# Attention with tokens as rows: the product in 64-row tiles, the norm per token on VectorE, x transposed afterwards

## The chip, the cores and the metric

The kernel runs on one core of a Trainium2 chip. The metric is device time in microseconds of one execution; the median of three runs is compared. A profiled execution gives the trace, whose times start at the first instruction. Engines are named as in the profile: PE is TensorE's matmuls, PEld its weight loads, DVE is VectorE, ACT ScalarE, POOL GpSimd, SP the engine that issues the loads and stores.

## The reference

q, k, v have the shape (8, 8, 576, 64): batch, heads, tokens, head dimension. A linear attention without softmax is followed by a root-mean-square norm per token and head, and then a feed-forward block with a gate over 4608 tokens x 512.

```python
kv = np.einsum('bhsd,bhse->bhde', k, v)
out = np.einsum('bhsd,bhde->bhse', q, kv)
rms = np.sqrt(np.mean(out * out, axis=-1, keepdims=True) + 1e-06)
x = (out / rms * g_norm).transpose(0, 2, 1, 3).reshape(B * S, H * D)
g = x @ w_gate                      # 512 -> 1536
result = (g / (1 + exp(-g)) * (x @ w_val)) @ w_out
```

## The kernel before

The 4608 tokens are cut into nine blocks of 512 (`BLK`), four tiles of 128 tokens each (`T`). A batch has 576 tokens, so block n takes its first tokens from batch n-1 and the rest from batch n. Features lie in four pairs of heads (`NS`), 128 rows each.

`Att` is the attention of a block, cut into steps. `load` asks for k and v of one batch (96 partitions, six chunks of 96 tokens) and q. `kv` computes k^T v of a pair of heads: six accumulating matmuls of 64 columns for the head u = 0, which writes PSUM rows 0 to 63, then six for u = 1, which writes rows 64 to 127 (L229). The result goes into a block-diagonal 128 x 128 matrix per pair (L235, L236). `turn_q` transposes q on TensorE, 16 transposes of 128 x 128 (L245), copied out by VectorE (L246). `product` multiplies with the block-diagonal matrix as the weight and 512 tokens as the moving operand (L257), so x comes out with features as rows. ScalarE squares it (L263), VectorE copies it (L264), and a matmul with the 0/1 matrix `head_of` sums the squares of each head into 8 rows (L265). `rms` computes 1/sqrt on 8 x 512 numbers in eleven VectorE instructions (L273 to L285: one scaling, a first guess from the bits, and three Newton steps of three). `scale` spreads the roots, times the gain, over 128 rows by a matmul with 8 rows (L291), and VectorE multiplies (L292). `sums` prepares four sums and differences for `Up`.

The feed-forward block is a seven-product scheme (`Quad`, L332, 256 columns a matmul): `Up` runs six times a block (7 x 4 matmuls each), `Down` once (7 x 12 matmuls). GpSimd prepares differences of weights (L120) and products (L121). Block 0 runs plain matmuls instead (`plain_up` L495, `plain_down` L508), as the weights arrive and are rounded from 64-bit words by ScalarE and VectorE meanwhile (L151 to L164).

All matmuls share one in-order stream on TensorE. Block n+1's attention steps are handed to block n's feed-forward as fillers: the `kv` steps between turns of `Up`, `turn_q` after `Up`, and one of the late steps after each part of `Down`:

```python
            ffn.up(kv)
            for step in kv + turn:
                step()
            ffn.down(late)
```

Block 0's own attention comes first, with only the first weight pieces beside it. The framework plans each engine's order from the program's order, with a cost for each instruction: an instruction whose inputs the plan expects late lets later ones go ahead of it. On the chip, each engine then runs its list in that order. PSUM has eight banks: two each for the pools a, b, c (products of `Quad`) and m (all of the attention).

A float32 matmul shows in the trace as two records, a transpose as one.

Of the kernel before, what the change touches and what calls it, by code (L numbers as in the profile page):

```python
# [18 lines left out]
def kernel(  # L19
# [51 lines left out]
    KT = S // KP  # L71
    eps = 1e-6
# [3 lines left out]
    def pool(name, bufs, **kw):  # L76
        return ctx.enter_context(tc.tile_pool(name=name, bufs=bufs, **kw))

    consts = pool("consts", 1)
    ld_pool = pool("ld", 7)  # L80
    qt_pool = pool("qt", 1)
    sq_pool = pool("sq", 2)
    st_pool = pool("st", 1)
    x_pool = pool("x", 1)
    h_pool = pool("h", 1)
    s_pool = pool("s", 1)
# [2 lines left out]
    o_pool = pool("o", 1)  # L89

    PS = bass.MemoryType.PSUM
    a_psum = pool("a_psum", 2, space=PS)
    b_psum = pool("b_psum", 2, space=PS)
    c_psum = pool("c_psum", 2, space=PS)
    m_psum = pool("m_psum", 2, space=PS)

    ident = consts.tile([P, P], F32, name="ident")
    make_identity(nc, ident)

    head_of = consts.tile([P, NS, H], F32, name="head_of")  # L100
    nc.vector.memset(head_of, 0.0)

    gain = consts.tile([H, NS, P], F32, name="gain")
    nc.vector.memset(gain, 0.0)
    for h in range(H):
        j, u = divmod(h, 2)
        rows = slice(u * D, (u + 1) * D)
        nc.vector.memset(head_of[rows, j, h : h + 1], 1.0)
        nc.gpsimd.dma_start(out=gain[h : h + 1, j, rows], in_=g_norm.rearrange("(o d) -> o d", o=1))

    kvs = [consts.tile([P, NS, P], F32, name=f"kv{i}") for i in range(3)]
    for t in kvs:
        nc.gpsimd.memset(t, 0.0)

    wg = consts.tile([P, NS, FF], F32, name="wg")
    wv = consts.tile([P, NS, FF], F32, name="wv")
# [4 lines left out]
    mul = lambda e, o, a, b: e.tensor_tensor(out=o, in0=a, in1=b, op=OP.mult)  # L121
# [67 lines left out]
    class Att:  # L189


        def __init__(self, n):
            self.n = n
            self.cut = 16 * n

        def load(self):
            n, cut = self.n, self.cut
            self.k, self.v, self.q = [], [], []
            if n < B:
                for j in range(NS):  # L200
                    hs = slice(2 * j, 2 * j + 2)
                    for tiles, src in ((self.k, k), (self.v, v)):
                        t = ld_pool.tile([P, 2 * BLK], F32, name="ld")
                        t = t[0:KP, 0 : 2 * KT * D].rearrange("p (h x) -> p h x", h=2)
                        nc.sync.dma_start(
                            out=t, in_=src[n, hs].rearrange("h (p t) d -> p h (t d)", t=KT)
                        )
                        tiles.append(t.rearrange("p h (t d) -> p h t d", t=KT))
            for i in range(2):
                hs = slice(4 * i, 4 * i + 4)  # L210
                t = ld_pool.tile([P, 2 * BLK], F32, name="ld")
                t = t.rearrange("p (t h d) -> p t h d", t=T, h=4)
                for b, s0, p0, p1 in ((n - 1, S - 4 * cut, 0, cut), (n, 0, cut, P)):
                    if p1 > p0:
                        rows = q[b, hs, s0 : s0 + T * (p1 - p0), :].rearrange("h (p t) d -> p t h d", t=T)
                        for c in range(T):
                            nc.sync.dma_start(out=t[p0:p1, c], in_=rows[:, c])
                self.q.append(t)

        def kv(self, js):  # L220
            if self.n == B:
                return
            if js[0] == 0:
                self.kv_ps = m_psum.tile([P, NS, D], F32, name="m")
            for j in js:
                for u in range(2):
                    rows = slice(u * D, (u + 1) * D)
                    for c in range(KT):
                        nc.tensor.matmul(  # L229
                            self.kv_ps[rows, j, :], lhsT=self.k[j][:, u, c, :], rhs=self.v[j][:, u, c, :],  # L230
                            start=(c == 0), stop=(c == KT - 1),
                        )
            if js[-1] == NS - 1:
                dst, ps = kvs[self.n % 3], self.kv_ps
                nc.scalar.copy(out=dst[0:D, :, 0:D], in_=ps[0:D])  # L235
                nc.vector.tensor_copy(out=dst[D:P, :, D:P], in_=ps[D:P])  # L236

        def turn_q(self, js):
            if js[0] == 0:
                self.qt = qt_pool.tile([P, NS, T, P], F32, name="qt")  # L240
            for j in js:
                ps = m_psum.tile([P, T, P], F32, name="m")
                hs = slice(2 * (j % 2), 2 * (j % 2) + 2)
                for t in range(T):
                    nc.tensor.transpose(ps[:, t, :], self.q[j // 2][:, t, hs, :], ident)  # L245
                nc.vector.tensor_copy(out=self.qt[:, j], in_=ps)  # L246

        def product(self, js):
            n, cut = self.n, self.cut
            if js[0] == 0:  # L250
                self.x = x_pool.tile([P, NS, BLK], F32, name="x")
                self.r_ps = m_psum.tile([P, BLK], F32, name="m")
            for j in js:
                ps = m_psum.tile([P, T, P], F32, name="m")
                for b, p0, p1 in ((n - 1, 0, cut), (n, cut, P)):
                    if p1 > p0:
                        nc.tensor.matmul(  # L257
                            ps[:, :, p0:p1], lhsT=kvs[b % 3][:, j, :], rhs=self.qt[:, j, :, p0:p1],
                            start=True, stop=True,
                        )  # L260
                ps = ps.rearrange("p t c -> p (t c)")
                sq = sq_pool.tile([P, BLK], F32, name="sq")
                nc.scalar.activation(out=sq, in_=ps, func=ACT.Square)  # L263
                nc.vector.tensor_copy(out=self.x[:, j, :], in_=ps)  # L264
                nc.tensor.matmul(  # L265
                    self.r_ps[0:H, :], lhsT=head_of[:, j, :], rhs=sq, start=(j == 0), stop=(j == NS - 1)
                )

        def rms(self):


            z = st_pool.tile([H, BLK], F32, name="z")
            nc.vector.tensor_scalar(  # L273
                out=z, in0=self.r_ps[0:H, :], scalar1=1.0 / D, scalar2=eps, op0=OP.mult, op1=OP.add
            )
            y = st_pool.tile([H, BLK], F32, name="y")
            nc.vector.tensor_scalar(
                out=y.bitcast(I32), in0=z.bitcast(I32), scalar1=-0.5, scalar2=float(0x5F3759DF),
                op0=OP.mult, op1=OP.add,
            )  # L280
            a = st_pool.tile([H, BLK], F32, name="a")
            for _ in range(3):
                nc.vector.scalar_tensor_tensor(out=a, in0=y, scalar=-0.5, in1=y, op0=OP.mult, op1=OP.mult)
                nc.vector.tensor_tensor(out=a, in0=a, in1=z, op=OP.mult)
                nc.vector.scalar_tensor_tensor(out=y, in0=a, scalar=1.5, in1=y, op0=OP.add, op1=OP.mult)  # L285
            self.y = y

        def scale(self, js):
            for j in js:
                ps = m_psum.tile([P, BLK], F32, name="m")  # L290
                nc.tensor.matmul(ps, lhsT=gain[:, j, :], rhs=self.y, start=True, stop=True)  # L291
                nc.vector.tensor_tensor(out=self.x[:, j, :], in0=self.x[:, j, :], in1=ps, op=OP.mult)  # L292

        def sums(self):
            x = self.x
# [6 lines left out]
            sub(nc.vector, self.s4, a12, a21)  # L302

        def steps(self):
            lo, hi = (0, 1), (2, 3)
            kv = [lambda: self.kv(lo), lambda: self.kv(hi)]
            turn = [lambda: self.turn_q(lo), lambda: self.turn_q(hi)]
            late = [
                lambda: self.product(lo), lambda: self.product(hi), self.rms,
                lambda: self.scale(lo), lambda: self.scale(hi),  # L310
            ]
            return kv, turn, late + ([self.sums] if self.n else [])

# [4 lines left out]
    class Quad:  # L318


        def __init__(self, steps):
            self.steps = steps
            self.ps = {}
# [124 lines left out]
    class Ffn:  # L448
# [2 lines left out]
            self.h = h_pool.tile([P, NF, BLK], F32, name="h")  # L451

        def store(self, o, t):
            rows = out[BLK * self.n : BLK * (self.n + 1), :].rearrange("(p t) d -> p t d", t=T)
            nc.sync.dma_start(out=rows[:, t : t + 2, :], in_=o)

        def up(self, fill):
# [141 lines left out]
```

## Time and profile before

| | |
|---|---|
| median of 3 runs | 1233.29 us (1233.04 to 1233.48) |
| profiled execution | 1231.31 us, span 1229.5 us |
| PE busy | 1188.3 us (97%) |
| PEld busy | 911.1 us (74%) |
| DVE, ACT, POOL busy | 439.6, 242.0, 403.2 us |
| mean granted TensorE clock | 0.982 |
| DMA | 57.50 MB, mean 47 GB/s |

Busy time counts every moment in which an instruction of that engine runs. Matmuls are pipelined and their records overlap, so the distance between the starts of two records says what one of them costs the stream. "L229" is line 229 of the kernel. In a group's row stand the line, engine, operation, what is written and read, the shape and the number of records; then busy time and the mean length of one in ns; then the idle time of the engine before them and what ended it.

### The profile page before, as it was taken

The numbers are of one execution on the slowest core, as the hardware profiler recorded it, in microseconds if no ns is written. First come the engines' busy times: TensorE is split into PE (matmuls) and PEld (weight loads), VectorE is DVE, ScalarE is ACT, GpSimd is POOL, SyncE is SP. The second block draws the span as 40 slices with busy tenths as digits, with TensorE's granted clock in tenths as the row PEclk, the third lists the DMA queues.
The fourth block names the chain that finished last, engine by engine and source line by source line (L and its number), as shares of the span: only waits on it lengthen the run. The fifth ranks groups of instructions, "written<-read, shape, count | busy, mean of one in ns | idle before, by whom it ended". The sixth has DMA issues, their size and how long they took to land.

```text
span 1229.5 us, 13554 instructions
## 1 busy us (share of the span) xinstructions
PE 1188.3 (97%) x5504; PEld 911.1 (74%) x5504; DVE 439.6 (36%) x707; ACT 242.0 (20%) x414; POOL 403.2 (33%) x329
## 2 busy tenths in 40 slices
PE   5699999999999999999999999999999999999998
PEld 3144344887788868887888778877887788768887
DVE  3556865213511342225222442135123512352121
ACT  2134420221022201221122102210222022201210
POOL 2000110444234423451344224432444235324550
PEclk8599999999999999999999999999999999999999
DMA  9134550030003000210011000200030000000000
GB/s 288 45 120 140 182 148 17 1 92 20 4 32 92 20 1 35 66 38 10 35 45 49 20 35 19 75 20 18 18 79 1 1 35 1 1 1 35 1 1 35
DMA packets 69533, 57.50 MB, mean 47 GB/s; under 512 B 41056, under 2 KB 65632, under 8 KB 69472
## 3 DMA queue, kind: packets, MB, share of 16 engines
q1 hardware_dynamic: 69216, 56.64, 15.3%
q8 instruction: 44, 0.72, 0.2%
q14 instruction: 17, 0.14, 0.0%
q0 software_dynamic: 256, 0.00, 0.0%
HBM read 47.19 MB, written 9.44 MB: 46 GB/s over the span
## 4 chain that ended last, share of the span: by engine, by line
PE 83%; DVE 2%; POOL 1%; issue 0%; ACT 0%; POOLq 0%
PE b L332 41%; PE c L332 19%; PE a L332 10%; PE m L257 3%; PE m L291 2%; PE m L265 2%; PE m L229 2%; PE b L508 2%; PE m L245 1%; POOL t L120 1%; POOL h L121 1%; DVE qt L246 0%; DVE wv L119 0%; DVE u L119 0%; DVE wv L120 0%; DVE s L119 0%
## 5 line engine op out<-in xcount | busy, mean ns | idle before, releaser
L120 POOL TENSOR_TENSOR t<-wv 128x512 f32<-128x512 f32 x48 | 63.4, 1322 | 402.1 <-PE b L332 153.4
L120 POOL TENSOR_TENSOR t<-wg,wv 128x512 f32<-128x512 f32 x96 | 123.0, 1284 | 188.4 <-PE c L332 100.7
L120 POOL TENSOR_TENSOR t<-wo 128x512 f32<-128x512 f32 x72 | 91.3, 1268 | 149.9 <-PE c L332 99.8
L119 DVE TENSOR_TENSOR s<-h 128x256 f32<-128x256 f32 x48 | 20.4, 425 | 306.6 <-POOL h L121 306.6
L332 PE MATMUL b<-x,t 128*128 128x256 f32 x384 | 91.3, 381 | 0.8
L332 PE MATMUL b<-x,wg 128*128 128x256 f32 x384 | 92.0, 382 | 0.0
L332 PE MATMUL b<-x,wv 128*128 128x256 f32 x384 | 90.7, 379 | 0.0
L332 PE MATMUL b<-xs,t 128*128 128x256 f32 x384 | 90.7, 379 | 0.0
L332 PE MATMUL c<-xs,t 128*128 128x256 f32 x384 | 90.7, 379 | 0.0
L332 PE MATMUL c<-xs,wv 128*128 128x256 f32 x384 | 90.7, 379 | 0.0
L332 PE MATMUL a<-x,wg 128*128 128x256 f32 x384 | 90.7, 379 | 0.0
L332 PE MATMUL b<-wo,h 128*128 128x256 f32 x384 | 90.1, 382 | 0.0
L119 DVE TENSOR_TENSOR u<-c,u 128x512 f32<-128x512 f32 x96 | 66.0, 687 | 62.3 <-ACT u L375 62.2
L332 PE MATMUL b<-t,h 128*128 128x256 f32 x384 | 87.0, 383 | 0.8 <-ACT u L437 0.8
L332 PEld LDWEIGHTS b<-t,h 128*128 128x128 f32 x384 | 71.7, 190 | 21.0 <-issue 11.8
L332 PEld LDWEIGHTS b<-wo,h 128*128 128x128 f32 x384 | 70.8, 190 | 16.3 <-issue 7.0
L332 PEld LDWEIGHTS b<-x,t 128*128 128x128 f32 x384 | 72.3, 190 | 12.0 <-issue 2.5
L332 PEld LDWEIGHTS c<-xs,wv 128*128 128x128 f32 x384 | 73.0, 190 | 9.9
L332 PEld LDWEIGHTS b<-xs,t 128*128 128x128 f32 x384 | 73.0, 190 | 9.9
L332 PEld LDWEIGHTS b<-x,wv 128*128 128x128 f32 x384 | 73.0, 190 | 9.9
L332 PEld LDWEIGHTS c<-xs,t 128*128 128x128 f32 x384 | 73.0, 190 | 9.9
L332 PEld LDWEIGHTS a<-x,wg 128*128 128x128 f32 x384 | 73.0, 190 | 9.9
(79 smaller groups left out, 1537.3 us busy)
## 6 DMA issues: line engine op xcount, KB each, us to landing
ld<-in_k_dram SPq DMA_DIRECT2D x32, 288.0 KB, 3.6
ld<-in_v_dram SPq DMA_DIRECT2D x32, 288.0 KB, 3.1
out_dram<-o SPq DMA_DIRECT2D x18, 512.0 KB, 2.6
ld<-in_moe_w_gate_dram SPq DMA_DIRECT2D x12, 512.0 KB, 4.2
ld<-in_moe_w_val_dram SPq DMA_DIRECT2D x12, 512.0 KB, 3.7
ld<-in_moe_w_out_dram SPq DMA_DIRECT2D x12, 512.0 KB, 3.5
ld<-in_q_dram SPq DMA_DIRECT2D x16, 128.0 KB, 2.8
ld<-in_q_dram SPq DMA_DIRECT2D x16, 112.0 KB, 2.7
```

Source lines behind the costliest of these rows:

```text
L119: add = lambda e, o, a, b: e.tensor_tensor(out=o, in0=a, in1=b, op=OP.add)
L120: sub = lambda e, o, a, b: e.tensor_tensor(out=o, in0=a, in1=b, op=OP.subtract)
L121: mul = lambda e, o, a, b: e.tensor_tensor(out=o, in0=a, in1=b, op=OP.mult)
L229: nc.tensor.matmul(self.kv_ps[rows, j, :], lhsT=self.k[j][:, u, c, :], rhs=self.v[j][:, u, c, :], start=(c == 0), stop=(c == KT - 1),)
L245: nc.tensor.transpose(ps[:, t, :], self.q[j // 2][:, t, hs, :], ident)
L257: nc.tensor.matmul(ps[:, :, p0:p1], lhsT=kvs[b % 3][:, j, :], rhs=self.qt[:, j, :, p0:p1], start=True, stop=True,)
L265: nc.tensor.matmul(self.r_ps[0:H, :], lhsT=head_of[:, j, :], rhs=sq, start=(j == 0), stop=(j == NS - 1))
L291: nc.tensor.matmul(ps, lhsT=gain[:, j, :], rhs=self.y, start=True, stop=True)
L332: nc.tensor.matmul(self.ps[name][:, e], lhsT=lhsT, rhs=rhs, start=first and (e, i) == (0, 0), stop=i == self.steps - 1, skip_group_check=True,
L508: nc.tensor.matmul(ps, lhsT=self.h[:, f, P * t : P * (t + 1)], rhs=wo[:, f, :], start=(f == 0), stop=(f == NF - 1),)
```

## The change

In the new form the product is made with tokens as rows. The transposed q of one tile and pair is the weight: 64 rows (one head's features) x 128 tokens; k^T v of that head, 64 x 64, is the moving operand. The heads u = 0 and u = 1 take rows 0 to 63 and 64 to 127, alternate, and write into different PSUM banks. In an odd block the tile in which two batches meet is cut into two halves of 64 tokens. The block's two halves (two tiles each) are worked on one after the other. ScalarE squares, VectorE sums 64 numbers per token and head (`tensor_reduce`), computes the root on 128 x 16 numbers and multiplies. Then x is transposed on TensorE and copied out of PSUM by ScalarE, which applies the gain per row. The matrices `head_of` and the spread gain, their matmuls, the block-diagonal zeros and the copies of x by VectorE are gone. In `kv`, the two heads alternate instruction by instruction. Every second copy of the transposed q goes to ScalarE; the copy of k^T v is one ScalarE instruction. A tile is now 128 consecutive tokens instead of every fourth, so q's loads are 4 or 5 a block, each for all heads, and the store writes rows of 2 KB. Pool a has one bank, pool m three.

```diff
-    st_pool = pool("st", 1)
+    st_pool = pool("st", 2)
+    xt_pool = pool("xt", 2)
...
-    a_psum = pool("a_psum", 2, space=PS)
+    a_psum = pool("a_psum", 1, space=PS)
...
-    m_psum = pool("m_psum", 2, space=PS)
+    m_psum = pool("m_psum", 3, space=PS)
...
-    head_of = consts.tile([P, NS, H], F32, name="head_of")
-    nc.vector.memset(head_of, 0.0)
-
-    gain = consts.tile([H, NS, P], F32, name="gain")
-    nc.vector.memset(gain, 0.0)
-    for h in range(H):
-        j, u = divmod(h, 2)
-        rows = slice(u * D, (u + 1) * D)
-        nc.vector.memset(head_of[rows, j, h : h + 1], 1.0)
-        nc.gpsimd.dma_start(out=gain[h : h + 1, j, rows], in_=g_norm.rearrange("(o d) -> o d", o=1))
-
-    kvs = [consts.tile([P, NS, P], F32, name=f"kv{i}") for i in range(3)]
-    for t in kvs:
-        nc.gpsimd.memset(t, 0.0)
+    gain = consts.tile([P, 1], F32, name="gain")
+    for u in range(2):
+        nc.gpsimd.dma_start(out=gain[u * D : (u + 1) * D], in_=g_norm.rearrange("(d o) -> d o", o=1))
+
+    kvs = [consts.tile([P, NS, D], F32, name=f"kv{i}") for i in range(3)]
...
-            self.cut = 16 * n
+
+            self.cut, half = divmod(n, 2)
+            self.split = half * D
+
+        def parts(self, t):
+
+            n, first = self.n, P * t - D * self.n
+            if t < self.cut:
+                return [(n - 1, S + first, 0, P)]
+            if t == self.cut and self.split:
+                return [(n - 1, S - D, 0, D), (n, 0, D, P)]
+            return [(n, first, 0, P)]
...
-                hs = slice(4 * i, 4 * i + 4)
-                t = ld_pool.tile([P, 2 * BLK], F32, name="ld")
-                t = t.rearrange("p (t h d) -> p t h d", t=T, h=4)
-                for b, s0, p0, p1 in ((n - 1, S - 4 * cut, 0, cut), (n, 0, cut, P)):
-                    if p1 > p0:
-                        rows = q[b, hs, s0 : s0 + T * (p1 - p0), :].rearrange("h (p t) d -> p t h d", t=T)
-                        for c in range(T):
-                            nc.sync.dma_start(out=t[p0:p1, c], in_=rows[:, c])
-                self.q.append(t)
+                ld = ld_pool.tile([P, 2 * BLK], F32, name="ld").rearrange("p (t h d) -> p t h d", t=2, h=H)
+                for t in range(2):
+                    for b, s0, p0, p1 in self.parts(2 * i + t):
+                        nc.sync.dma_start(
+                            out=ld[p0:p1, t], in_=q[b, :, s0 : s0 + p1 - p0, :].rearrange("h p d -> p h d")
+                        )
+                    self.q.append(ld[:, t].rearrange("p (j u) d -> p j (u d)", u=2))
...
             for j in js:
-                for u in range(2):
-                    rows = slice(u * D, (u + 1) * D)
-                    for c in range(KT):
+                for c in range(KT):
+                    for u in range(2):
                         nc.tensor.matmul(
-                            self.kv_ps[rows, j, :], lhsT=self.k[j][:, u, c, :], rhs=self.v[j][:, u, c, :],
-                            start=(c == 0), stop=(c == KT - 1),
+                            self.kv_ps[u * D : (u + 1) * D, j, :], lhsT=self.k[j][:, u, c, :],
+                            rhs=self.v[j][:, u, c, :], start=(c == 0), stop=(c == KT - 1),
                         )
-                dst, ps = kvs[self.n % 3], self.kv_ps
-                nc.scalar.copy(out=dst[0:D, :, 0:D], in_=ps[0:D])
-                nc.vector.tensor_copy(out=dst[D:P, :, D:P], in_=ps[D:P])
...
+                nc.scalar.copy(out=kvs[self.n % 3], in_=self.kv_ps)
+
+        def turn_q(self, i):
+
+            if i == 0:
+                self.qt = qt_pool.tile([P, T, NS, P], F32, name="qt")
+            for t in (2 * i, 2 * i + 1):
+                ps = m_psum.tile([P, NS, P], F32, name="m")
+                for j in range(NS):
+                    nc.tensor.transpose(ps[:, j], self.q[t][:, j], ident)
+                if t % 2:
+                    nc.scalar.copy(out=self.qt[:, t], in_=ps)
+                else:
+                    nc.vector.tensor_copy(out=self.qt[:, t], in_=ps)
+
+        def product(self, i):
+
+
+
+
+            ps = [m_psum.tile([P, 2, NS, D], F32, name="m") for _ in range(2)]
+            for t in range(2):
+                for j in range(NS):
+                    for b, _, p0, p1 in self.parts(2 * i + t):
+                        for u in range(2):
+                            rows = slice(u * D, (u + 1) * D)
+                            nc.tensor.matmul(
+                                ps[u][p0:p1, t, j, :], lhsT=self.qt[rows, 2 * i + t, j, p0:p1],
+                                rhs=kvs[b % 3][rows, j, :], start=True, stop=True,
+                            )
+            z = st_pool.tile([P, 2, 2, NS], F32, name="z")
+            for u in range(2):
+                sq = sq_pool.tile([P, 2, NS, D], F32, name="sq")
+                nc.scalar.activation(out=sq, in_=ps[u], func=ACT.Square)
+                nc.vector.tensor_reduce(out=z[:, u], in_=sq, axis=mybir.AxisListType.X, op=OP.add)
+            y = self.root(z)
+            xt = xt_pool.tile([P, 2, NS, 2, D], F32, name="xt")
+            for u in range(2):
+                mul(nc.vector, xt[:, :, :, u], ps[u], y[:, u].unsqueeze(3).to_broadcast([P, 2, NS, D]))
+            self.xt = xt
+
...
+        def root(self, z):
+
+            nc.vector.tensor_scalar(out=z, in0=z, scalar1=1.0 / D, scalar2=eps, op0=OP.mult, op1=OP.add)
+            y = st_pool.tile([P, 2, 2, NS], F32, name="y")
...
+            return y
+
+        def turn_x(self, i):
+            if i == 0:
+                self.x = x_pool.tile([P, NS, BLK], F32, name="x")
+            xt = self.xt.rearrange("p t j u d -> p t j (u d)")
+            for j in range(0, NS, 2):
+                ps = m_psum.tile([P, 2, 2, P], F32, name="m")
+                for e in range(2):
+                    for t in range(2):
+                        nc.tensor.transpose(ps[:, e, t], xt[:, t, j + e], ident)
+                nc.scalar.activation(
+                    out=self.x[:, j : j + 2, HB * i : HB * (i + 1)], in_=ps.rearrange("p e t c -> p e (t c)"),
+                    func=ACT.Copy, scale=gain,
+                )
...
-            lo, hi = (0, 1), (2, 3)
-            kv = [lambda: self.kv(lo), lambda: self.kv(hi)]
-            turn = [lambda: self.turn_q(lo), lambda: self.turn_q(hi)]
+            kv = [lambda: self.kv((0, 1)), lambda: self.kv((2, 3))]
+            turn = [lambda: self.turn_q(0), lambda: self.turn_q(1)]
             late = [
-                lambda: self.product(lo), lambda: self.product(hi), self.rms,
-                lambda: self.scale(lo), lambda: self.scale(hi),
+                lambda: self.product(0), lambda: self.turn_x(0), lambda: self.product(1), lambda: self.turn_x(1),
             ]
...
-            rows = out[BLK * self.n : BLK * (self.n + 1), :].rearrange("(p t) d -> p t d", t=T)
+            rows = out[BLK * self.n : BLK * (self.n + 1), :].rearrange("(t p) d -> p t d", t=T)
             nc.sync.dma_start(out=rows[:, t : t + 2, :], in_=o)
```

More of the change, by code (lines that the diff above doesn't have):

```diff
@@ L193, in __init__ @@
             self.n = n
-            self.cut = 16 * n
+            self.cut, half = divmod(n, 2)
[7 more added lines that the diff above has]
+            return [(n, first, 0, P)]
         def load(self):
-            n, cut = self.n, self.cut
+            n = self.n
             self.k, self.v, self.q = [], [], []
@@ L232, in kv @@
                         )
             if js[-1] == NS - 1:
-                dst, ps = kvs[self.n % 3], self.kv_ps
-                nc.scalar.copy(out=dst[0:D, :, 0:D], in_=ps[0:D])
-                nc.vector.tensor_copy(out=dst[D:P, :, D:P], in_=ps[D:P])
[L238 to L276, printed above, removed]
+                nc.scalar.copy(out=kvs[self.n % 3], in_=self.kv_ps)
[10 more added lines that the diff above has]
+                    nc.vector.tensor_copy(out=self.qt[:, t], in_=ps)
@@ L280, in rms @@
             )
-            a = st_pool.tile([H, BLK], F32, name="a")
+            a = st_pool.tile([P, 2, 2, NS], F32, name="a")
             for _ in range(3):
@@ L285, in rms @@
                 nc.vector.scalar_tensor_tensor(out=y, in0=a, scalar=1.5, in1=y, op0=OP.add, op1=OP.mult)
[L286 to L292, printed above, removed]
+            return y
[12 more added lines that the diff above has]
+                )
         def sums(self):
```

## The prediction

> **What bounds the kernel now.** I read the page first: busy time by engine, then the chain that ended last.
>
> ```profile
> span 1229.5 us, 13554 instructions
> ...
> PE 1188.3 (97%) x5504; PEld 911.1 (74%) x5504; DVE 439.6 (36%) x707; ACT 242.0 (20%) x414; POOL 403.2 (33%) x329
> ...
> PE b L332 41%; PE c L332 19%; PE a L332 10%; PE m L257 3%; PE m L291 2%; PE m L265 2%; PE m L229 2%; PE b L508 2%; PE m L245 1%; POOL t L120 1%; POOL h L121 1%; DVE qt L246 0%; DVE wv L119 0%; DVE u L119 0%; DVE wv L120 0%; DVE s L119 0%
> ```
>
> TensorE is the bound and the end chain runs on it. So an edit is worth the TensorE time that it takes out of the stream, plus the waits it ends or makes. In the groups by shape, k^T v's row has 768 records for 8 x 48 matmuls: a matmul is two records here, a transpose one.
>
> ```profile
> L229 PE MATMUL m<-ld 96*64 96x64 f32 x768 | 44.6, 237 | 8.4 <-DMA ld<-in_v_dram 8.3
> ```
>
> Records overlap, so their price is the distance between starts. The timeline of TensorE (start, length, line): three rows with block 1's attention, then block 3's matmuls while block 4's attention is fed in.
>
> ```profile
> 182.90 1.02 PE L265 MATMUL m<-sq,head_of 128*8 128x512 f32 x2
> 183.85 1.24 PE L257 MATMUL m<-qt,kv 128*128 128x64 f32 x4
> 184.93 1.02 PE L508 MATMUL b<-wo,h 128*128 128x512 f32 x2
> ...
> 504.00 2.48 PE L229 MATMUL m<-ld 96*64 96x64 f32 x48
> 506.40 1.99 PE L332 MATMUL b<-x,wg 128*128 128x256 f32 x8
> ...
> 549.83 0.82 PE L245 MATMUL m<-ident,ld 128*128 128x128 f32 x6
> 550.48 1.03 PE L332 MATMUL b<-wo,h 128*128 128x256 f32 x4
> 552.62 0.66 PE L245 MATMUL m<-ident,ld 128*128 128x128 f32 x4 [1.11 <-DVE qt L246]
> 553.12 4.48 PE L332 MATMUL b<-wo,h 128*128 128x256 f32 x20
> 557.44 1.03 PE L257 MATMUL m<-qt,kv 128*128 128x256 f32 x4
> 558.30 1.03 PE L332 MATMUL c<-t,s 128*128 128x256 f32 x4
> 559.26 1.02 PE L265 MATMUL m<-sq,head_of 128*8 128x512 f32 x2
> ...
> 581.13 1.98 PE L291 MATMUL m<-y,gain 8*128 8x512 f32 x4
> 583.04 5.45 PE L332 MATMUL b<-t,h 128*128 128x256 f32 x24
> ```
>
> A 256-column record costs 0.216 us (553.12 to 557.44, over 20). A transpose costs 0.109 (549.83 to 550.48, over 6). And a change of array shape costs about 0.1: the four records from 558.30, ahead of 8-column ones, take 0.96 where 4 x 0.216 is due. I charge it on entering and on leaving.
>
> **The change part by part.** The sum is made against the profiled execution, 1231.3 us (span 1229.5); the median of the runs is 1233.3, 2 us above it. Blocks 1 to 8 have their attention beside other matmuls; block 0's stands alone and is costed last.
>
> Head sums and spreading go. A block pays 4 x 0.95 for head_of (182.90 to 183.85, with the change out), 4 x 0.1 for the change in, 2 x 1.91 for gain (581.13 to 583.04) and 2 x 0.2 for the changes there: 8.4 us, times 8: **-67**.
>
> The product is recut. Today's four groups cost about 0.9 each (0.86 from 557.44 to 558.30), 3.6 a block, 29 in 8 blocks. The new form issues 32 matmuls a block, 64 records of 64 columns, each behind its own load of 64 rows x 128 columns. In odd blocks one 128-token tile is halved: 48 such records and 32 with 64-column loads. For nine blocks that is 512 + 128, for blocks 1 to 8 it is 448 + 128. No row has such a record. The nearest from below is a transpose, which also hangs on a 128-column load: 0.109. From above: the four records from 183.85 are two of 64 columns and two of 448 (the split of block 1), 1.08 together; at 0.216 per 256 columns the larger two take 0.76, so the small ones 0.16 each. One after another I take 0.109, as the 0.16 includes the step from one bank's work to the next, and 0.058 for a 64-column load with 64 columns moved, which is what L229 does. There the trace shows two tiles of the array at work at once. In the first 48-record run, records in flight within one head, and at the change of head:
>
> ```profile
> 504.31:504.32 0.01, 0.01 (x4) 1.00 0.00 0
> 504.72:504.73 0.01, 0.01 (x7) 1.00 0.00 0
> ```
>
> A record lasts 237 ns, so four in flight is one per 0.058 us; seven is nearly twice that, for the few records in which the queue already reaches the next head. The new product alternates between the upper and lower 64 rows, into different PSUM banks. That these overlap too is not in the trace: the two heads of L229 differ in columns, not rows. I take half the serial price, because the queue already feeds two tiles: 448 x 0.0545 + 128 x 0.029 = 28, plus 0.4 a block for shape changes, 31. Net **+2**. The ends are this and the serial price, +32 over nine blocks (at 0.16 a load +58).
>
> Transposing x back is new: 16 transposes a block, 16 x 0.109 x 8 = **+14**.
>
> k^T v by alternating heads. A run of 48 records takes 2.40 us (504.00 to 506.40). If the two heads overlap throughout, as they now do at the change, it takes 24 x 0.058 + 0.15 of tail = 1.55, so 0.85 less, twice a block, for blocks 1 to 7: **-12**. The ends: 0 if the queue doesn't reach across, -14.
>
> The wait in turning q. From 550.48 to 552.62 stand four records worth 0.86; the other 1.28 is a wait, whose chain reads
>
> ```profile
> 549.68 1.24 POOL h L121
> ...
> 551.97 0.61 DVE qt L246
> ```
>
> So the copy that frees the bank sits in VectorE's queue behind additions that wait for GpSimd's product. The change sends every second copy to ScalarE and gives m three banks instead of two, so the fourth tile needs the bank of the first, whose copy is not behind them. That wait goes in blocks 1 to 8: 8 x 1.28 = **-10**, with 0 as the other end. The price is an m bank taken from a_psum: the a tile is read within a step and next written after six more, so one bank costs nothing unless that read is over 10 us late.
>
> New waits. A half of x now runs product, Square, reduce, root, multiply, transpose, with these prices:
>
> ```profile
> L263 ACT ACTIVATE sq<-m 128x512 f32<-128x512 f32 x36 | 21.5, 596 | 104.5 <-PE m L257 104.5
> ```
>
> ```profile
> L292 DVE TENSOR_TENSOR x<-x,m 128x512 f32<-128x512 f32 x36 | 23.6, 682 | 7.8 <-PE m L291 7.8
> ```
>
> ```profile
> L101 DVE MEMSET head_of<- 128x32 f32 x1 | 0.1, 85 | 0.8 <-PEq L582 0.8
> ```
>
> Two Squares are 1.2, the last reduce 0.7 (taken as L292), two multiplies 1.4. The eleven steps of the root work on 16 columns instead of 512: between the 0.085 of the 32-column memset and the 0.68 that they take on 512 columns (the row of L292 has the like); I take 0.1, nearest the memset in size, so 1.1. Together 4.4 us from product to transpose. Between these steps the program lays a part of Down, 24 records or 5.2 us, and the order is planned with such times in view. VectorE is in order, and one of Down's long subtractions, or an addition behind GpSimd, can stand ahead. I take 1 us a block, like the wait just removed: **+8**; ends 0 and 16 x 4.4 = 70.
>
> At nothing: the scaling copies out of PSUM move to ScalarE (20% busy), VectorE loses the copies of the product and the root on 512 columns (its part of the idle 7.69 us at 51.93 below) and gains four reduces and two small roots; q comes in 4 or 5 larger transfers instead of 8 to 16 on SP's queue, asked for a whole block ahead; GpSimd loses three memsets and six gain transfers that stand under the first load. The stores go out in 2 KB pieces instead of 4 KB: only the last is on the path, and a microsecond there lies within the range.
>
> The start. Until 59 us TensorE mostly waits, at a lowered clock:
>
> ```profile
> 20.00:30.00 10.00, 4.56 (x8) 0.96 (x6) 8.57 (x18) 5.13 (x9) 0.00 (x0) 0.67 1.09 379
> 30.00:40.00 10.00, 8.06 (x9) 1.50 (x10) 5.68 (x12) 2.48 (x5) 0.00 (x0) 0.50 0.50 159
> ```
>
> (PE, PEld, DVE, ACT, POOL busy, then clock), and the chain by the timeline is
>
> ```profile
> 21.17 2.08 PE L257 MATMUL m<-qt,kv 128*128 128x512 f32 x2 [0.57 <-DVE qt L246]
> ...
> 29.84 2.08 PE L257 MATMUL m<-qt,kv 128*128 128x512 f32 x2 [4.18 <-DVE x L264]
> ...
> 51.93 7.16 PE L291 MATMUL m<-y,gain 8*128 8x512 f32 x8 [7.69 <-issue]
> 59.02 3.78 PE L495 MATMUL b<-x,wg 128*128 128x512 f32 x4
> ```
>
> Four products share one free bank, then the root on 512 columns and the spreading. New: from 21.2 a half costs its product at half clock (3.5), 4.4 of chain, eight transposes at half clock (1.7) and two copies (1.2), 10.8; the second half's product overlaps, so some 7.5 more: 40, against 59.0: **-19**. Ends: both halves in series with VectorE's rounding of the first weights (8.6 busy of 10 us) between, 52, so -7; and -26.
>
> Sum: -67 + 2 + 14 - 12 - 10 + 8 - 19 = -84. 1231.3 - 84 = 1147, with the 2 us to the median **1149**. By the ends of start and waits the case spans 1132 to 1165.
>
> **The rivals.**
> Serial loads: upper and lower rows don't overlap, every record waits for its load. For it: no row shows row tiles at once, and the transposes' 0.109 may be their load's. Against: 7 in flight. Then 512 x 0.0545 + 128 x 0.029 = 32 more: 1181. [...]
>
> k^T v does not gain, that is, the alternation does nothing because each head's accumulation keeps the queue in order: +12, 1161. Against it: those same seven.
>
> New waits: the chain stands half exposed at each of the 16 half-blocks, because VectorE is held by GpSimd at the wrong moment as at 551.97: 16 x 2.2 = 35 in place of 8: 1176; fully, 70: 1211. For it: the trace has one such wait a block. Against: all other planned waits of the block are hidden.
>
> Slower: row-tile records expose their whole load and drain. A record of L229 lasts 237 ns from start to end; if each new one had to end before the next load begins, it would cost that and the load's 0.109, 0.35. The point where it decides: the product's 31.6 would have to grow by 84, to 0.2 us a record (512 x 0.2 + 128 x 0.1 = 115). At 0.35 it would be 1149 + 192 - 32 = 1309. Against: the transposes come every 0.109 us with a 128-column load each, so loads are hidden behind the record before.
>
> **How the numbers follow.** Forecast 0.52; k^T v without gain 0.08; serial loads 0.21; exposed chain 0.13; slower 0.04; gains and losses cancelling 0.02. Out of 1129 to 1188 fall the upper half of the exposed chain, the slower and the cancelling cases, and some 0.06 below, when the start gives its full end and no new wait comes. About 0.2% (2.5 us) can be told apart here: faster 0.94, within it 0.02, slower 0.04.
>
> **What would show it.** Right: no 8-column or 8-row matmuls; the 48-record runs at about 1.6 us; products (16 matmuls a half) at about 1.75 us with six or more records in flight; the wait of L245 on the qt copy gone; first L495 near 40 us; blocks some 9 us shorter. Wrong: product halves of 3.5 us or more (serial); transposes of xt waiting on the multiply by over 1 us each; the first weights' rounding holding x until 50; the late part of block 0, where VectorE is full, eating what block 1 gains.

## The result and the profile after

The changed kernel takes 1191.81 us (median of four runs; 1188.76 to 1193.08) against 1233.16 us for the kernel before in four runs beside it: a ratio of 0.9665, interval 0.9641 to 0.9689. It is faster by 41 us, half of the 84 that were forecast, and it lies above the forecast's range. The profiled execution is 1190.74 us, 40.6 below that of before. The page of the changed kernel, with span, busy times, and the chain that ended last:

```profile
span 1189.0 us, 14539 instructions
...
PE 1122.0 (94%) x6016; PEld 919.8 (77%) x6016; DVE 404.4 (34%) x770; ACT 274.5 (23%) x468; POOL 401.7 (34%) x320
...
PE b L339 43%; PE c L339 18%; PE a L339 8%; PE b L515 3%; PE m L259 3%; DVE y L286 2%; PE m L297 2%; PE m L228 2%; DVE z L267 1%; PE m L242 1%; DVE xt L112 1%; DVE y L278 1%; ACT sq L266 1%; DVE a L284 1%; DVE a L285 1%
```

TensorE's busy time fell by 66 us, but the span only by 40: TensorE now waits. In the chain of before no VectorE line had 1%. Now L286, the last instruction of a Newton step on 128 x 16 numbers, has 2%, beside L267, L278, L284 and L285.

TensorE's timeline of the changed kernel, block 3's matmuls with block 4's attention fed in (start, length, line; in brackets the idle time before and what ended it):

```profile
478.32 1.62 PE L228 MATMUL m<-ld 96*64 96x64 f32 x48
479.87 1.99 PE L339 MATMUL b<-x,wg 128*128 128x256 f32 x8
...
522.44 1.25 PE L242 MATMUL m<-ident,ld 128*128 128x128 f32 x10
523.53 5.35 PE L339 MATMUL b<-wo,h 128*128 128x256 f32 x24
528.80 2.00 PE L259 MATMUL m<-kv,qt 64*128 64x64 f32 x32
530.74 5.45 PE L339 MATMUL c<-t,s 128*128 128x256 f32 x24
539.79 1.30 PE L297 MATMUL m<-ident,xt 128*128 128x128 f32 x8 [3.61 <-DVE xt L112]
540.89 6.84 PE L339 MATMUL b<-wo,h 128*128 128x256 f32 x24
547.65 2.00 PE L259 MATMUL m<-kv,qt 64*128 64x64 f32 x32
549.58 5.45 PE L339 MATMUL a<-wo,h 128*128 128x256 f32 x24
555.43 1.06 PE L297 MATMUL m<-ident,xt 128*128 128x128 f32 x8 [0.40 <-DVE xt L112]
556.34 5.35 PE L339 MATMUL b<-t,h 128*128 128x256 f32 x24
```

What was forecast for the matmuls is there: k^T v in 1.55 us (478.32 to 479.87; 2.40 before), half a product in 1.94 (528.80 to 530.74), and transposes of q with no wait. The loss is at 539.79. Twenty-four records from 530.74 are worth 5.27 us (as from 523.53 to 528.80); the first transposes of x come 9.05 us after them, so TensorE loses 3.78. The second half's transposes (549.58 to 555.43) lose 0.58. And the 24 records from 540.89 take 6.76, 1.49 too much, and the eight transposes ahead of them 1.10, where those from 555.43 take 0.91. For this the windows of the trace give the reason (each row has the engines' busy time, then the granted clock in front of DMA share and GB/s):

```profile
540.50:543.90 3.40, 3.40 (x12) 2.74 (x11) 0.00 (x0) 1.31 (x2) 0.00 (x0) 0.50 0.00 0
543.90:547.30 3.40, 3.40 (x17) 3.01 (x16) 0.00 (x0) 0.00 (x0) 0.00 (x0) 1.00 0.00 0
```

For 3.4 us, from soon after the long wait, TensorE has half its clock, which costs 1.7. Waits and clock together cost 3.78 + 0.58 + 1.7 = 6.1 us in this block. Of the seven such blocks one has a first wait of 3.26 instead of 3.78, and another no second wait; the clock dips in all seven. Together they lose 41 us, where the prediction had 8. Why the chain is late stands in VectorE's timeline, the root of that half, and in GpSimd's beside it:

```profile
532.78 0.17 DVE L276 TENSOR_SCALAR z<-z 128x16 f32<-128x16 f32 x1
532.99 1.18 DVE L278 TENSOR_SCALAR y<-z 128x16 int32<-128x16 int32 x1
...
534.62 1.28 DVE L286 SCALAR_TENSOR_TENSOR y<-a,y 128x16 f32<-128x16 f32 x1
...
536.36 1.27 DVE L286 SCALAR_TENSOR_TENSOR y<-a,y 128x16 f32<-128x16 f32 x1
```

```profile
532.88 1.26 POOL L111 TENSOR_TENSOR t<-wo 128x512 f32<-128x512 f32 x1 [6.95 <-PE c L339]
534.60 1.26 POOL L111 TENSOR_TENSOR t<-wo 128x512 f32<-128x512 f32 x1 [0.46 <-PE c L339]
536.33 1.26 POOL L111 TENSOR_TENSOR t<-wo 128x512 f32<-128x512 f32 x1 [0.46 <-PE c L339]
```

Eight of the eleven root steps take 0.17 to 0.18 us. Three take 1.2 to 1.3, each begun just after a GpSimd subtraction, and each ending as it ends: about 3.2 us lost, of a wait of 3.78. In the second half GpSimd is idle, all eleven take 0.17 to 0.18, and the chain of 5.85 us (549.58 to 555.43) is only 0.58 longer than the 5.27 us of its cover.

The start: TensorE's timeline of the changed kernel, and VectorE's in the middle of the first long wait.

```profile
18.45 2.13 PE L259 MATMUL m<-kv,qt 64*128 64x64 f32 x32
35.20 1.94 PE L297 MATMUL m<-ident,xt 128*128 128x128 f32 x8 [14.62 <-DVE xt L112]
37.07 3.68 PE L259 MATMUL m<-kv,qt 64*128 64x64 f32 x32
46.53 1.94 PE L297 MATMUL m<-ident,xt 128*128 128x128 f32 x8 [5.78 <-DVE xt L112]
48.39 5.66 PE L502 MATMUL b<-x,wg 128*128 128x512 f32 x8
```

```profile
31.08 0.17 DVE L286 SCALAR_TENSOR_TENSOR y<-a,y 128x16 f32<-128x16 f32 x1
31.16 0.42 DVE L145 TENSOR_SCALAR u<-u 128x512 f32<-128x512 f32 x1
31.50 0.17 DVE L284 SCALAR_TENSOR_TENSOR a<-y 128x16 f32<-128x16 f32 x1
```

The first plain matmul of `plain_up` starts at 48.39 (59.02 before, 40 forecast). Between two root steps VectorE's list holds one or two instructions of the weights' rounding (L145 here), so the first half's transposes come 14.8 us after its product. The second half's product begins only behind them, and its chain follows alone.

The ledger of the profiled executions: start -10.6; block 0's `Down`, with block 1's attention, 67.06 to 58.73, so -8.3; the other blocks -21.7; sum -40.6.

### The profile page after: what moved, and what is told of

Read it like the earlier page. It is cut to its first block, busy times and chain, and to the rows that moved or that the text cites. A ratio compares the mean times of both kernels' runs of the same rounds, so it can differ in the third digit from the quotient of the medians.

```text
span 1189.0 us, 14539 instructions
## 1 busy us (share of the span) xinstructions
PE 1122.0 (94%) x6016; PEld 919.8 (77%) x6016; DVE 404.4 (34%) x770; ACT 274.5 (23%) x468; POOL 401.7 (34%) x320
## 4 chain that ended last, share of the span: by engine, by line
PE 79%; DVE 7%; issue 1%; ACT 1%; DMA 0%; DVEq 0%
PE b L339 43%; PE c L339 18%; PE a L339 8%; PE b L515 3%; PE m L259 3%; DVE y L286 2%; PE m L297 2%; PE m L228 2%; DVE z L267 1%; PE m L242 1%; DVE xt L112 1%; DVE y L278 1%; ACT sq L266 1%; DVE a L284 1%; DVE a L285 1%
## 5 line engine op out<-in xcount | busy, mean ns | idle before, releaser
L111 POOL TENSOR_TENSOR t<-wv 128x512 f32<-128x512 f32 x48 | 66.3, 1382 | 395.9 <-PE b L339 170.7
L339 PE MATMUL b<-wo,h 128*128 128x256 f32 x384 | 94.6, 406 | 0.0
L339 PEld LDWEIGHTS b<-wo,h 128*128 128x128 f32 x384 | 78.5, 208 | 12.0 <-POOL h L112 0.3
```

Of the source, the lines that this page charges most:

```text
L111: sub = lambda e, o, a, b: e.tensor_tensor(out=o, in0=a, in1=b, op=OP.subtract)
L339: nc.tensor.matmul(self.ps[name][:, e], lhsT=lhsT, rhs=rhs, start=first and (e, i) == (0, 0), stop=i == self.steps - 1, skip_group_check=True,
```

## The experiments

The runs of the kernel before give 1231.2 us beside the first four experiments and 1230.0 and 1230.1 beside the others, where they gave 1233.2 beside the changed kernel. So the changed kernel is carried over by its ratio: 1189.9 us beside the first four, 1188.7 beside the rest.

Two theories for the blocks. A: GpSimd's subtractions stretch VectorE's small steps; move them apart and the waits go, with the clock's dips behind them. B: the chain is simply longer than its cover (eleven dependent steps, ScalarE and VectorE queues), whatever GpSimd does. For the start, S1: rounding that stands between the root's steps; S2: the second product waits for the two m banks of the first.

**Without the subtractions of that place.** In `Down`, a tile already there is used in place of the one that GpSimd would make.

```diff
-                    down.turn_t(7)
+                    down.t[7] = down.t[5]
```

> The changed kernel without GpSimd's three subtractions for Down's product 7 (it uses the tiles of product 5 instead, so that part of the output is another sum). Theory A: the wait of the first x transposes (3.77 us a block) comes from VectorE's root steps standing still while GpSimd's subtraction t<-wo runs (three of eleven take 1.2 us instead of 0.175). Then all eleven take 0.175, the first wait falls to about 0.5 us like that of the second half, the half-clock stretch behind it goes, and the time is near 1191 - 7 x (3.2 + 1.5) = 1158. Theory B: the chain is simply longer than the 5.2 us part of Down laid over it. Then the wait stays above 2 us and the time above 1175. Theory C, for the clock: the dips come from the small shapes and not from the wait. Then seven dips remain whatever the wait does, about 10 us: 1168.

Measured: 1155.08 us in one run, 34.8 below the changed kernel's 1189.9. Its TensorE timeline, both transposes of x:

```profile
525.65 1.07 PE L297 MATMUL m<-ident,xt 128*128 128x128 f32 x8 [0.40 <-DVE xt L112]
...
539.61 1.07 PE L297 MATMUL m<-ident,xt 128*128 128x128 f32 x8 [0.40 <-DVE xt L112]
```

All root steps take 0.17 to 0.18, the first wait falls to that of the second, and the 24 records behind it keep the full clock (5.28 us from 526.55 to 531.83, and no dip in any of the seven blocks; the mean granted clock is 0.988, against 0.976). The chain is the same program; B would have kept its wait. The small shapes are the same too, so theory C would have kept its dips.

**One part of Down more as cover.**

```diff
-                lambda: self.product(0), lambda: self.turn_x(0), ...
+                lambda: self.product(0), lambda: None, lambda: self.turn_x(0), ...
```

> One empty step between the first product and its x transposes, so that two parts of Down (10.4 us) lie over the first half's chain of 9 us; nothing else is changed. Theories A and B both: the first wait goes, the second (0.57) stays, and with it the dips, as no pause is over 1 us: 1191 - 7 x (3.77 + 1.5) = 1154. Theory C: the dips remain, 1165. If the wait were a mere symptom and the time lost elsewhere: 1185 or more.

Measured: 1170.01 us, ratio 0.9505 (0.9488 to 0.9522): 16 above the expectation. The first wait is gone, but the second half's root now stands one part of `Down` later. VectorE, GpSimd and TensorE there:

```profile
550.05 1.24 DVE L285 TENSOR_TENSOR a<-a,z 128x16 f32<-128x16 f32 x1
551.33 1.19 DVE L286 SCALAR_TENSOR_TENSOR y<-a,y 128x16 f32<-128x16 f32 x1
```

```profile
550.00 1.27 POOL L111 TENSOR_TENSOR t<-wv 128x512 f32<-128x512 f32 x1 [15.55 <-PE b L339]
551.23 2.49 POOL L111 TENSOR_TENSOR t<-wg,wv 128x512 f32<-128x512 f32 x2
```

```profile
554.06 1.06 PE L297 MATMUL m<-ident,xt 128*128 128x128 f32 x8 [2.48 <-DVE xt L112]
```

The collision moved: other subtractions, those for the next `Up`, stretch two other steps, now of the second root, by 2.1 us together, and the second wait grows from 0.58 to 2.66. That is A again, at a place that the expectation had left out.

**More tiles for the subtractions**, so that GpSimd could make them earlier.

```diff
-    xt_pool = pool("xt", 2)
+    xt_pool = pool("xt", 1)
...
-    t_pool = pool("t", 6)
+    t_pool = pool("t", 9)
```

> Nine tiles for the weight differences instead of six (and one xt tile instead of two, for room). The orders of TensorE, VectorE and ScalarE stay the same; only GpSimd's subtractions can start earlier, as they needn't wait for a tile of product 5. Theory A: the three subtractions stand ahead of the root or meet it once at most; root steps of 1.2 us fall from three to one or none in the first half, the wait from 3.8 to 0.5 to 1.7 us: 1155 to 1165. If the earlier subtractions meet the second half's root instead, that wait grows by as much: 1175 to 1190. Theory B: no change, 1188 to 1193.

Measured: 1189.35 us, ratio 0.9664 (0.9647 to 0.9681): no change. The subtractions for `Down` did go earlier, but three of the next `Up`'s (t<-wv, t<-wg), from 534.31 on, took their place, since they are released by the same product of TensorE, and the first wait is again 3.79 us. The expectation failed. Of the theories it says only that whichever subtraction stands there has the same effect.

**The two heads of the product one after the other**, for the price of the row tiles.

```diff
-            for t in range(2):
-                for j in range(NS):
-                    for b, _, p0, p1 in self.parts(2 * i + t):
-                        for u in range(2):
+            for u in range(2):
+                for t in range(2):
+                    for j in range(NS):
+                        for b, _, p0, p1 in self.parts(2 * i + t):
```

> The product with the head u as the outer loop, so that neighbouring matmuls use the same 64 rows of the array; the same instructions, no alternation. If the alternation of row tiles is what makes a half's 32 records take 1.93 us, they now take about 3.6 (0.109 each and the shape changes): 16 halves x 1.7 = 27 more, 1218. If records of 64 rows come every 0.055 us anyway, 1191.

Measured: 1219.94 us in one run. Its TensorE timeline:

```profile
540.96 3.39 PE L259 MATMUL m<-kv,qt 64*128 64x64 f32 x32
544.28 5.45 PE L339 MATMUL c<-t,s 128*128 128x256 f32 x24
...
560.57 3.39 PE L259 MATMUL m<-kv,qt 64*128 64x64 f32 x32
563.89 7.13 PE L339 MATMUL a<-wo,h 128*128 128x256 f32 x24
570.86 1.04 PE L297 MATMUL m<-ident,xt 128*128 128x128 f32 x8
```

Half a product takes 3.32 us (540.96 to 544.28) in place of 1.94, and 16 halves x 1.38 are 22 of the 30 us lost against the changed kernel. There is also a second dip of the clock in each of the seven blocks: the 24 records from 563.89 are worth 5.27 us and take 6.97, with no wait ahead of them, only 3.3 us in which half of the array's rows worked at a time; the mean granted clock is 0.963, against 0.976 in the changed kernel. Seven of these make 12 us. The waits are shorter here (3.16 for 3.78, none for 0.58), which gives most of that back, and some microseconds stay unassigned.

**Another order**, drawn from these four: the first product one part of `Down` later, the second right behind the first transposes, and its transposes two parts after it.

```diff
-                lambda: self.product(0), lambda: self.turn_x(0), lambda: self.product(1), lambda: self.turn_x(1),
+                lambda: None, lambda: self.product(0), lambda: (self.turn_x(0), self.product(1)), lambda: None, lambda: self.turn_x(1),
```

> The late steps moved in Down: product of the first half one part later (behind product 5, whose matmuls release the tiles that let GpSimd subtract), its x transposes and the second product behind product 6, the second x transposes behind product 7. Theory A (VectorE's root steps stand still only while GpSimd's subtractions run, and GpSimd is idle in products 6 and 2): all root steps 0.175 us, first wait 0.5 us or a little more, second none, no half-clock stretches in the blocks: 1152 to 1160, like the kernel without the three subtractions. If GpSimd's work follows the root wherever it is put: 1175 to 1190.

Measured: 1155.11 us (1154.26 to 1155.3), ratio 0.9393 (0.9378 to 0.9409), with no work left out: 33.6 below the changed kernel's 1188.7. GpSimd's last subtraction, the first root's first and last step, and TensorE:

```profile
523.63 1.27 POOL L111 TENSOR_TENSOR t<-wo 128x512 f32<-128x512 f32 x1 [0.46 <-PE c L339]
```

```profile
527.39 0.17 DVE L276 TENSOR_SCALAR z<-z 128x16 f32<-128x16 f32 x1
...
529.49 0.17 DVE L286 SCALAR_TENSOR_TENSOR y<-a,y 128x16 f32<-128x16 f32 x1
```

```profile
531.11 1.09 PE L297 MATMUL m<-ident,xt 128*128 128x128 f32 x8 [0.32 <-DVE xt L112]
532.13 2.41 PE L259 MATMUL m<-kv,qt 64*128 64x64 f32 x32
534.47 5.45 PE L339 MATMUL a<-wo,h 128*128 128x256 f32 x24
```

The subtractions end at 524.9, the root begins at 527.4 and lasts 2.3 us, instead of 5.5 from 532.78 on. What is left is a wait of 0.3 to 0.5 us and 0.4 in the second product (2.34 for 1.94), which now follows the first transposes at once; it may have to wait for the banks that the first multiplies free, but that is not shown. A run of the same kernel beside the last experiment:

> The same order without the two edits of the start, beside the run with them: 1154 to 1156 us, first plain matmuls of Up at about 48 us.

Measured: 1155.18 us (1154.77 to 1155.67), ratio 0.9395 (0.9379 to 0.9411).

**k^T v alone**, the alternation of heads put into the kernel before.

```diff
-                for u in range(2):
-                    rows = slice(u * D, (u + 1) * D)
-                    for c in range(KT):
+                for c in range(KT):
+                    for u in range(2):
+                        rows = slice(u * D, (u + 1) * D)
```

> The kernel before with the alternation of heads in k^T v alone. If the two heads' matmuls overlap when they alternate, each of 14 runs of 48 records falls from 2.40 to 1.55 us: -12, and up to 2 more in block 1, 1219 to 1222. If the alternation does nothing by itself: 1233.

Measured: 1218.56 us, ratio 0.9912 (0.9897 to 0.9926), so -11.4 for a forecast of -12, and the interval lies clear of 1. Its TensorE timeline:

```profile
499.94 1.62 PE L229 MATMUL m<-ld 96*64 96x64 f32 x48
501.48 1.99 PE L332 MATMUL b<-x,wg 128*128 128x256 f32 x8
```

**The start, attention ahead of the rounding** in the program, with the same loads ahead of both.

```diff
-    weights(4)
+    while loaded < 5:
+        load_w(*pieces[loaded])
+        loaded += 1
     for steps in blocks[0].steps():
         for step in steps:
             step()
+    weights(4)
```

> At the start, block 0's attention stands ahead of the rounding of the first four weight pieces in the program (the pieces are still asked for first). Theory S1: the first half's x is late by the rounding that stands between its steps in VectorE's queue (14.8 us from product to transposes). Then this falls to about 6 us, the first plain matmul comes at 39 to 42 us instead of 48.4, and the time is 1183 to 1186. Theory S2: the second half's product waits for the first's two PSUM banks, and that decides: at most 2 us gained, as the rounding then stands ahead of the plain matmuls instead.

Measured: 1185.36 us, ratio 0.964 (0.9626 to 0.9655), 3.3 below 1188.7: the time as expected, the place not. The first plain matmul comes at 44.3, not 39 to 42; from the first product's end to its transposes it is still 10.6 us (14.8 in the changed kernel), because VectorE's list, which the framework orders by its plan, keeps some rounding between the root's steps.

**The start, banks of b and c for block 0's second product.**

```diff
-            ps = [m_psum.tile([P, 2, NS, D], F32, name="m") for _ in range(2)]
+            pools = (b_psum, c_psum) if self.n == 0 and i else (m_psum, m_psum)
+            ps = [p.tile([P, 2, NS, D], F32, name=p.name[0]) for p in pools]
```

> Block 0's second product writes into free banks of the pools b and c, so it needn't wait for the first half's multiplies. Theory S2: the product starts at 20 us instead of 37, its chain follows the first's on VectorE, first plain matmul at 42 to 44 us, 1185 to 1187. Theory S1: the rounding decides, the chain of both halves fills VectorE until 44 us or more, gain 0 to 3 us.

Measured: 1182.72 us (1180.27 to 1187.39), ratio 0.9624 (0.96 to 0.9648), 6.0 below 1188.7 and faster than expected. The second product now runs beside the first, all 16 transposes follow each other from 39.87, and the first plain matmul stands at 43.7. So S1 and S2 both hold: the first plain matmul comes 4.1 us earlier by the one edit and 4.7 by the other. These places show it better than the times: the intervals of both ratios still overlap with that of the changed kernel (0.9641 to 0.9689). They are good to about a microsecond, as the two runs of the other order, whose start is unchanged, have that matmul at 49.2 and 47.9.

**Order and both edits of the start together.**

> The order of the run in which product 0 starts one step later and the second product comes right behind the first transposes, with both edits of the start: block 0's attention is laid ahead of the first weights' rounding, and its second product writes into banks of b and c. If the blocks keep their gain (first wait about 0.5 us, no second one) and both edits of the start gain by themselves, 1155 - 5 - 8 = 1142 us; if they gain the same time, since VectorE's rounding of the weights sets the end of either, 1146 to 1150. First plain matmuls of Up after 40 us in the first case, 43 in the second (48.4 in the changed kernel).

Measured: 1146.28 us (1144.66 to 1148.0), ratio 0.9322 (0.9307 to 0.9337): 8.9 below the same order alone, run beside it. Its TensorE timeline has the first plain matmul at 40.0:

```profile
40.03 5.04 PE L503 MATMUL b<-x,wg 128*128 128x512 f32 x8
```

That is 8.4 us earlier than in the changed kernel, and 4.1 and 4.7 make 8.8: within that microsecond the two edits add up, as do their single gains of 3.3 and 6.0 us. By its place this is the first of the two cases, though the time lies at the edge of the second: the first case's 1142 us was worked out from the times of different sets without carrying them over, and so is 4 too low. This version beats both kernels.

## Why the prediction was half right

**Head sums, product, transposes, k^T v: right.** Half a product took 1.94 us where 1.75 and the change of shape were forecast, and 3.32 with the heads in series: the rival "serial loads" is refuted by that difference. k^T v is settled by the run that has it alone. The head sums and the transposes of x were not taken alone; for them only the sum speaks. The blocks gained 30.0 us, and with the 41 of waits and clock put back it is 71, where the forecast's terms other than the new waits make 73.

**The wait in turning q: right.** L242's row at 522.44 shows ten records in 1.09 us, none waiting; 1.28 us a block are gone.

**New waits: the step that failed.** The prediction put 1 us a block, +8, for a chain of 4.4 us under 5.2 us of cover, a price taken over from another wait and not worked out; it measured about 6 us a block, 41 us in seven. The sign of being wrong that the prediction named came true: transposes of xt that wait over 1 us (539.79). Three parts of the term were off. The root steps were priced at 0.1 us from a memset and take 0.17, with starts 0.21 apart; so the bare chain is longer than its cover (5.85 us), and 0.58 remains even where nothing disturbs it. Then the three stretched steps, 3.2 us. Then the clock behind the long wait, 1.7 us, which was in no case of the forecast. The runs without the subtractions and with the other order, both at 1155 us, get 34 to 35 us back of these.

The rival "New waits" had named VectorE held by GpSimd, but as at 551.97: a copy queued behind an addition that waits for GpSimd's result. What happened is not a queue: the steps have begun and run seven times as long. Its 16 exposures of 2.2 us, 35 in all, are near the 41 measured by chance; the true ones are six of 3.8 and one of 3.3, with a clock dip each, and six of 0.58. And the span of 1132 to 1165 that the prediction gives for the ends of start and waits does not follow from those ends: with new waits at their bad end of 70 alone, 62 more than forecast, it is 1211.

The profile before had the sign. Its groups by line and shape, two with the same operation and size, and its timeline of VectorE and of GpSimd at two places:

```profile
L120 DVE TENSOR_TENSOR xs<-x 128x512 f32<-128x512 f32 x16 | 17.9, 1121 | 0.5
...
L119 DVE TENSOR_TENSOR xs<-x 128x512 f32<-128x512 f32 x8 | 5.5, 692 | 0.3
```

```profile
546.01 0.69 DVE L246 COPY qt<-m 128x512 f32<-128x512 f32 x1 [1.34 <-PE m L245]
546.62 0.68 DVE L119 TENSOR_TENSOR u<-c,u 128x512 f32<-128x512 f32 x1
...
592.61 1.68 DVE L120 TENSOR_TENSOR xs<-x 128x512 f32<-128x512 f32 x1
```

```profile
545.68 1.27 POOL L120 TENSOR_TENSOR t<-wo 128x512 f32<-128x512 f32 x1 [2.07 <-PE m L245]
...
592.47 1.27 POOL L120 TENSOR_TENSOR t<-wv 128x512 f32<-128x512 f32 x1 [1.85 <-PE b L332]
```

The two groups work on SBUF alone: 1121 ns and 692 for the same work, and 692 to 1675 ns from one instruction of the first group to the next. The slow one at 592.61 begins inside a GpSimd subtraction. The two instructions from 546.01 read PSUM (m, c) and run at 0.69 and 0.68 with GpSimd busy beside them. The root itself ran undisturbed before, from 572.4 to 580.0 in block 3, as GpSimd was idle from 568.2 to 586.9; the change puts it among the subtractions. Beside a subtraction, instructions with all operands in SBUF took 1.27 us for 0.17 (L286) and 1.68 for 0.69 (L120), and the two that read PSUM 0.69 and 0.68. L278, at 1.18 for 0.17, has only one input. Why VectorE is held up is not shown; the runs show that the stretch follows GpSimd's subtractions to whichever root step they meet: L278 and L286 in the changed kernel, L285 and L286 with more cover.

**The start: right in sign, half in size.** -10.6 for -19. The forecast took the second half's product as overlapped and the chain at 4.4; it left the rounding between the root steps to the bad end (52). The measured 48.4 lies inside the ends given, nearer the bad one. The run with order and both start edits reaches 40.0, and its ratio makes 1149.7 of the 1233.29 us: the forecast's place and its time, but only with the program changed.

The blocks miss the forecast by 35 us (-30.0 for -65); waits and clock explain 41 - 8 = 33. The start misses it by 8.4. Two us stay unassigned.

## What to carry to other kernels

A chain of small VectorE steps is planned by its place, not only by its length: look in GpSimd's timeline for what runs while it runs. In this kernel steps on SBUF alone took 1.18 to 1.28 us for 0.17 beside GpSimd's subtractions on SBUF: keep the two apart, or reorder until they are. Before pricing a step, compare groups of the same operation and size; two means far apart (1121 and 692 ns) can be a contention that already exists. And when a wait of some 3 us on TensorE is at stake, count the slower matmuls after it too (here 1.7 us behind a wait of 3.78).

## What was not expected of the hardware

- A VectorE instruction on 128 x 16 numbers in SBUF took 0.17 us, and in the root's chain one started every 0.21 us; beside a GpSimd subtraction on 128 x 512 it took 1.18 to 1.28 us.
- Row tiles of 64 x 128 overlapped: 32 records took 1.94 us alternating, 3.32 in series.
- The granted clock was 0.50 for about 3.4 us after the first wait of all seven blocks of the changed kernel (TensorE idle for 3.08 to 3.61 us). In the run with more cover, whose waits are shorter (2.48 us at 554.06), it was 0.66 from 306 to 311 us and 1.00 from 554 to 558. In the run with heads in series, 24 records with no wait ahead of them took 6.97 us for 5.27, after 3.3 us of half the array's rows. What exactly sets the dip off stays open.
- The clock's row seems to miss a dip: in the last experiment it reads 1.00 at the start, where eight transposes took 1.9 us, as long as in the changed kernel at 0.50; at a full clock eight took 0.91 (from 555.43). Here the distance between records says more than the row.
